# Shifting every right-side SBUF tile of an attention and two-layer kernel by 96 bytes

## The chip, the cores and the metric

The kernel runs on one core of one Trainium2 chip. The metric is the device time of one execution in microseconds (us). Three runs of the kernel before gave 1021.41, 1022.04 and 1022.06 us; the median is 1022.04 us. The profile is of one further execution.

## The reference

The inputs are q, k, v of 4 batches, 8 heads, 576 positions and 64 channels, a vector s per head and position, and two pairs of weights of 512 x 2048 and 2048 x 512. The weights are float64, all else float32, the output too.

```python
cum  = cumsum(max(s, 0))
bias = min(-(cum[:, None] - cum[None, :]), 0)
attn = softmax(where(causal, -1e9, q @ k.T / 8 + bias))
x = (attn @ v) as [2304, 512]
h = x @ w1_in;  x = max(0.01*h, h) @ w1_out            # first layer
h = x @ w2_in;  out = (max(h,0) + log1p(exp(-|h|))) @ w2_out   # second layer
```

## The kernel before

**Attention.** `attention` goes through 16 pairs of heads. TensorE makes scores (L252, L262), VectorE masks them and takes maxima (L281), ScalarE exponentiates (L295), GpSimd divides by the sums (L306), TensorE transposes (L318, L323) and multiplies with V (L354). The result stands in SBUF as `xh` and `xl`: a value rounded to the type that TensorE reads in one pass (float32r), and what the rounding left over. Beside it `Fill` already does part of the first layer for batches whose attention is done, with 288 tokens a chunk (L143 through `h_mm`, L539).

**The two layers.** The main loop at the end takes `steps`: the layer, a group of four blocks of 128 hidden units, a chunk of tokens (512, 512, 256, 512, 512; in the very first group twice 288), and one block `f`. Each step has two parts on TensorE:

- `h_mm` (L143) makes 128 hidden units for the chunk: four slices of the model width, three products each (`hi` with `xh`, `hi` with `xl`, `lo` with `xh`). These 12 matmuls add up in one bank of PSUM. The stationary operand is a weight tile (`wih`, `wil`), the moving one `xh` or `xl`.
- `out_mm` (L651) of three steps earlier multiplies the activations `gh` and `gl` with `woh` and `wol` into four banks of PSUM. In layer 0 the weights are stationary and `gh`, `gl` move (`ops = outs[i][:, :N], ((wh[:, sl], gh), ...`); in layer 1 it is the other way round: a slice of 128 columns of `gh` or `gl` is stationary and the 512 columns of `woh` or `wol` move. A step of 512 tokens has 12 such matmuls, in layer 1 a step of 256 tokens has 6. The first product of two halves goes first, then, with `low`, the four with `gl`.

Between the two ScalarE, VectorE and GpSimd make `gf`, `gh` and `gl` of the hidden units (L605, L610 to L624, L149, L150). They also split the next weights into `hi` and `lo` (`split_w`, L105 to L130). Program order on each engine is the order in which the Python code issues. `later` and `tick` put a piece off by so many half steps.

**Where tiles lie.** A tile pool is a piece of every SBUF partition. Pools without a side are laid upwards from the first free byte, 16,512, which is 129 x 128; pools with `side="right"` are laid downwards from the last one, 229,344, which is 1791 x 128 + 96. All pools here are multiples of 128 bytes long (but for the small `st` tiles on the left), so every left tile of the table starts at a multiple of 128 and every right one at 96 past one.

| tile | side | starts at (bytes) | past a multiple of 512 |
|---|---|---|---|
| `xh`, `xl` | left | 16,512 and 53,376 | 128 |
| `wih`, `wil`, `woh`, `wol` | left | 90,240 to 137,344 | 128 |
| `wm`, `wt` of the weight split | left | 139,392 to 145,536 | 128 |
| `acc` (sum of the layer) | left | 155,776 | 128 |
| `gf`, `t`, `e`, `l` (two layers) | right | 196,576 to 210,912 | 480 |
| `gh`, `gl` (two layers), 4 each | right | 212,960 to 227,296 | 480 |
| `gf`, `o`, `gh`, `gl` of `Fill`, 288 columns | right | 209,120 to 224,096 | 96, 224, 352 or 480 |
| `rawi`, `rawo` during attention; `c0`, `c1`, `bb` at the start | right | 217,056 to 225,248 | 480 or 224 |

A chunk of `xh` starts at a multiple of 1024 bytes within its slice in all steps of 512 or 256 tokens; in the chunks of 288 tokens it starts at multiples of 1152. A slice of 128 columns is 512 bytes.

Of the kernel before, what the change touches and what calls it, by code (L numbers as in the profile page):

```python
# [9 lines left out]
F32 = mybir.dt.float32  # L10
# [7 lines left out]
P = 128  # L18
# [12 lines left out]
def attn_moe_moe(ctx, tc, q, k, v, s, w1i, w1o, w2i, w2o, out):  # L31
# [18 lines left out]
    def pool(name, bufs=1, **kw):  # L50
        return tc.tile_pool(name=name, bufs=bufs, **kw)

    dram = ctx.enter_context(pool("dram", space=bass.MemoryType.DRAM))
    keep = ctx.enter_context(pool("keep"))


    xh = keep.tile([P, KD, NT], F32R, tag="xh", name="xh")
    xl = keep.tile([P, KD, NT], F32R, tag="xl", name="xl")
# [688 lines left out]
```

## Time and profile before

| what | value |
|---|---|
| median of three runs | 1022.04 us |
| span of the profiled execution, first to last instruction | 1020.2 us |
| outside the span (median less span) | 1.8 us |
| TensorE busy (matmuls) | 992.0 us, 97% |
| GpSimd, ScalarE, VectorE busy | 559.2, 536.8, 506.3 us |
| main loop of the two layers | from 276 us on; layer 1's output matmuls from 614 us on |

The span is what the profiler recorded between the first and the last instruction. The time of a run also holds what lies around it. Matmuls overlap in TensorE: one begins before the one ahead of it has ended. So the mean duration of a group is longer than its pace; the pace is read from the starts of matmuls that follow each other in the timeline.

### The profile page before, as it was taken

What the parts mean: (1) busy time and instruction counts of PE and PEld (TensorE: products, weight loads), DVE (VectorE), ACT (ScalarE), POOL (GpSimd) and SP (SyncE); (2) the same over time, 40 slices, a digit from 0 to 9 for tenths busy, and PEclk for the clock granted to TensorE, in tenths of its full rate; (3) what the DMA queues carried; (4) which work ended last, traced back from release to release, by engine and by line L of the source; (5) the groups of instructions that cost most, each with busy time, mean ns of one, the idle gap of its engine ahead of it and who ended that gap; (6) DMA issues with size and microseconds to landing.
All of it is one profiled execution on the core that took longest, in us unless ns stands there. A gap on an engine that the chain in (4) does not pass through costs nothing.

```text
span 1020.2 us, 15105 instructions
## 1 busy us (share of the span) xinstructions
PE 992.0 (97%) x5498; PEld 812.4 (80%) x5498; DVE 506.3 (50%) x1133; ACT 536.8 (53%) x1152; POOL 559.2 (55%) x565
## 2 busy tenths in 40 slices
PE   7889999999999999999999998999999999999998
PEld 4667788888998888888888887888778877888886
DVE  6886665554021312321244158547575767576443
ACT  4877676656355333432444365666645554565452
POOL 6757455434156335533553356667766676667453
PEclk9999999999999999999999999999999999999999
DMA  5422333210252002100220021101210121010202
GB/s 172 135 97 67 113 106 101 93 59 25 73 205 76 22 1 83 63 21 1 83 62 22 16 68 41 42 2 45 80 42 1 42 82 42 1 42 21 83 22 83
DMA packets 38518, 62.04 MB, mean 61 GB/s; under 512 B 2932, under 2 KB 25972, under 8 KB 38444
## 3 DMA queue, kind: packets, MB, share of 16 engines
q1 hardware_dynamic: 38204, 60.74, 18.2%
q8 instruction: 44, 0.72, 0.3%
q10 hardware_dynamic: 240, 0.33, 0.1%
q14 instruction: 30, 0.25, 0.1%
HBM read 52.65 MB, written 8.40 MB: 60 GB/s over the span
## 4 chain that ended last, share of the span: by engine, by line
PE 73%; POOL 10%; DVE 8%; issue 6%; ACT 3%; DMA 0%; DVEq 0%; POOLq 0%; ACTq 0%
PE ps_h L143 30%; PE ps_out L651 27%; PE pt_v L354 4%; PE ps_o L539 4%; PE pt_s L262 4%; POOL t L619 3%; PE pt_t L323 3%; POOL gl L150 2%; POOL wm L120 2%; DVE wm L114 2%; PE pt_s L252 2%; ACT sc L295 1%; DVE wm L111 1%; DVE wm L117 1%; POOL wil L130 1%
## 5 line engine op out<-in xcount | busy, mean ns | idle before, releaser
L150 POOL TENSOR_TENSOR gl<-gf,gh 128x512 fp32r<-128x512 f32 (+2 forms) x148 | 178.3, 1206 | 258.9 <-ACT gh L149 243.4
L143 PE MATMUL ps_h<-xh,wih 128*128 128x512 f32 (+2 forms) x688 | 246.5, 358 | 1.1 <-ACT o L543 0.6
L143 PE MATMUL ps_h<-xl,wih 128*128 128x512 f32 (+2 forms) x688 | 244.7, 356 | 0.0
L143 PE MATMUL ps_h<-xh,wil 128*128 128x512 f32 (+2 forms) x688 | 243.9, 354 | 0.0
L143 PEld LDWEIGHTS ps_h<-xh,wih 128*128 128x128 f32 x688 | 129.4, 188 | 21.5 <-ACT o L543 0.8
L306 POOL TENSOR_SCALAR sc<-sc,st 128x512 f32<-128x512 f32 (+4 forms) x160 | 88.1, 562 | 103.8 <-DVE st L302 61.3
L143 PEld LDWEIGHTS ps_h<-xl,wih 128*128 128x128 f32 x688 | 129.4, 188 | 19.0
L143 PEld LDWEIGHTS ps_h<-xh,wil 128*128 128x128 f32 x688 | 129.4, 188 | 18.5
L662 DVE TENSOR_TENSOR acc<-ps_out,acc 128x512 f32<-128x512 f32 (+1 forms) x114 | 67.7, 655 | 129.1 <-PE ps_out L651 129.1
L149 ACT ACTIVATE gh<-gf 128x512 fp32r<-128x512 f32 (+2 forms) x148 | 85.3, 576 | 82.7 <-DVE gf L624 81.8
L605 ACT ACTIVATE gf<-ps_h 128x512 f32<-128x512 f32 (+2 forms) x68 | 36.7, 539 | 172.1 <-PE ps_h L143 168.2
L651 PE MATMUL ps_out<-woh,gh 128*128 128x512 f32 x288 | 116.2, 403 | 5.8 <-ACT gh L149 3.2
L624 DVE TENSOR_TENSOR gf<-gf,t 128x512 f32<-128x512 f32 (+1 forms) x80 | 56.0, 700 | 127.0 <-POOL t L619 127.0
L111 DVE TENSOR_SCALAR wm<-wm 128x512 f32<-128x512 f32 x64 | 42.1, 658 | 147.3 <-ACT wm L105 140.3
L651 PE MATMUL ps_out<-wol,gh 128*128 128x512 f32 x288 | 115.0, 399 | 0.0
L295 ACT ACTIVATE sc<-sc,st 128x512 f32<-128x512 f32 (+2 forms) x144 | 83.3, 581 | 42.9 <-DVE st L286 22.0
L120 POOL TENSOR_TENSOR wm<-wm,wt 128x512 int32<-128x512 int32 x64 | 88.1, 1377 | 28.0 <-DVE wm L117 28.0
L619 POOL TENSOR_TENSOR t<-e,t 128x512 f32<-128x512 f32 (+1 forms) x80 | 98.3, 1228 | 0.0
L651 PE MATMUL ps_out<-gh,woh 128*128 128x512 f32 (+2 forms) x272 | 97.1, 365 | 0.0
L651 PE MATMUL ps_out<-gh,wol 128*128 128x512 f32 (+2 forms) x272 | 96.6, 364 | 0.0
L281 DVE CUSTOM_DVE_ANT_0 sc<-pt_s,mask 128x512 f32<-128x512 f32 (+2 forms) x144 | 66.7, 480 | 57.2 <-PE pt_t L323 46.1
L651 PE MATMUL ps_out<-woh,gl 128*128 128x512 f32 x288 | 80.6, 397 | 1.2 <-POOL gl L150 1.1
(93 smaller groups left out, 1729.2 us busy)
## 6 DMA issues: line engine op xcount, KB each, us to landing
rawi<-in_moe_w_in SPq DMA_DIRECT2D x32, 512.0 KB
rawo<-in_moe_w_out SPq DMA_DIRECT2D x32, 512.0 KB
V<-in_v SPq DMA_DIRECT2D x16, 320.0 KB
Q<-in_q SPq DMA_DIRECT2D x15, 320.0 KB
K<-in_k SPq DMA_DIRECT2D x16, 288.0 KB
out<-acc SPq DMA_DIRECT2D x18, 256.0 KB
part<-o SPq DMA_DIRECT2D x24, 144.0 KB
acc<-part SPq DMA_DIRECT2D x6, 576.0 KB
```

The source lines that it names most:

```text
L111: nc.vector.tensor_scalar(mf, mf, D_MIN, D_MAX, op0=ALU.max, op1=ALU.min)
L120: nc.gpsimd.tensor_tensor(m, m, t, op=ALU.add)
L143: nc.tensor.matmul(ps, a, b, start=n == 0, stop=n == 3 * KD - 1)
L149: nc.scalar.activation(gh, gf, AF.Copy)
L150: nc.gpsimd.tensor_tensor(gl, gf, gh.bitcast(F32), op=ALU.subtract)
L281: nc.vector.tensor_tensor_reduce(out=self.sc[:, j, c], in0=self.ps[j][:, c], in1=m, scale=-scale, scalar=3.0e38, op0=ALU.add, op1=ALU.min, ...
L295: nc.scalar.activation(x, x, AF.Exp, scale=-1.0, bias=self.stat(0, e), accum_out=self.stat(1, e))
L306: nc.gpsimd.tensor_scalar(x, x, self.stat(2, e), 1.0, op0=ALU.mult, op1=ALU.mult)
L619: nc.gpsimd.tensor_tensor(t, e, t, op=ALU.subtract)
L624: nc.vector.tensor_tensor(gf, gf, t, op=ALU.add)
L651: nc.tensor.matmul(ps, a, b, start=f == 0 and m == 0, stop=f == G - 1 and m == 2)
L662: nc.vector.tensor_tensor(d, o, d, op=ALU.add)
```

## The change

A pool named `edge` is opened on the right side ahead of all others there, and one tile of 128 partitions x 24 float32 (96 bytes) is taken from it. Nothing reads or writes this tile. All later right-side tiles start 96 bytes lower: at multiples of 128. `gh` and `gl` of the two layers start at 384 past a multiple of 512 instead of 480; those of `Fill` at 0, 128, 256 or 384. Left-side tiles stay where they are. Every engine has the same instructions in the same order, with the same waits.

```diff
     dram = ctx.enter_context(pool("dram", space=bass.MemoryType.DRAM))
     keep = ctx.enter_context(pool("keep"))
-
+    edge = ctx.enter_context(pool("edge", side="right"))
+    edge.tile([P, 24], F32, tag="edge", name="edge")
 
     xh = keep.tile([P, KD, NT], F32R, tag="xh", name="xh")
```

## Rows read from the trace of the kernel before

**Rows 1.** The page: span, busy time by engine, the granted TensorE clock.
```profile
span 1020.2 us, 15105 instructions
PE 992.0 (97%) x5498; PEld 812.4 (80%) x5498; DVE 506.3 (50%) x1133; ACT 536.8 (53%) x1152; POOL 559.2 (55%) x565
PEclk9999999999999999999999999999999999999999
```

**Rows 2.** The page: the chain of waits, shares by engine.
```profile
PE 73%; POOL 10%; DVE 8%; issue 6%; ACT 3%; DMA 0%; DVEq 0%; POOLq 0%; ACTq 0%
```

**Rows 3.** Groups by line and shape, TensorE: count, busy us, mean ns, idle before.
```profile
L143 PE MATMUL ps_h<-xl,wih 128*128 128x512 f32 x448 | 175.4, 392 | 0.0
...
L651 PE MATMUL ps_out<-woh,gh 128*128 128x512 f32 x288 | 116.2, 403 | 5.8 <-ACT gh L149 3.2 <-DVE acc L662 2.1 <-ACT acc L660 0.5
L651 PE MATMUL ps_out<-wol,gh 128*128 128x512 f32 x288 | 115.0, 399 | 0.0
...
L651 PE MATMUL ps_out<-gh,woh 128*128 128x512 f32 x192 | 76.3, 398 | 0.0
...
L143 PE MATMUL ps_h<-xl,wih 128*128 128x256 f32 x112 | 31.6, 282 | 0.0
...
L651 PE MATMUL ps_out<-gh,wol 128*128 128x256 f32 x48 | 12.1, 283 | 0.0
```

**Rows 4.** Timeline of TensorE, a step of layer 0: start us, duration us.
```profile
522.00 0.40 PE L143 MATMUL ps_h<-xh,wih 128*128 128x512 f32 x1
...
524.07 0.39 PE L143 MATMUL ps_h<-xh,wih 128*128 128x512 f32 x1
...
524.75 0.40 PE L651 MATMUL ps_out<-gh,woh 128*128 128x512 f32 x1
...
527.57 0.40 PE L143 MATMUL ps_h<-xh,wih 128*128 128x512 f32 x1
```

**Rows 5.** Timeline of TensorE, a step of layer 1.
```profile
803.07 0.40 PE L143 MATMUL ps_h<-xh,wih 128*128 128x512 f32 x1
...
803.76 0.39 PE L143 MATMUL ps_h<-xh,wih 128*128 128x512 f32 x1
...
805.80 0.39 PE L651 MATMUL ps_out<-woh,gh 128*128 128x512 f32 x1
...
808.61 0.40 PE L143 MATMUL ps_h<-xh,wih 128*128 128x512 f32 x1
```

**Rows 6.** Timeline of TensorE, matmuls of 288 columns in `Fill` and just after.
```profile
263.10 0.29 PE L143 MATMUL ps_h<-xh,wih 128*128 128x288 f32 x1
...
267.90 0.30 PE L539 MATMUL ps_o<-gh,woh 128*128 128x288 f32 x1
...
270.40 0.29 PE L539 MATMUL ps_o<-gh,woh 128*128 128x288 f32 x1
...
272.00 0.30 PE L539 MATMUL ps_o<-gh,woh 128*128 128x288 f32 x1
...
277.59 0.29 PE L143 MATMUL ps_h<-xh,wih 128*128 128x288 f32 x1
...
282.33 0.29 PE L651 MATMUL ps_out<-gh,woh 128*128 128x288 f32 x1
...
283.91 0.29 PE L143 MATMUL ps_h<-xh,wih 128*128 128x288 f32 x1
```

**Rows 7.** Groups by line and shape, ScalarE and GpSimd.
```profile
L149 ACT ACTIVATE gh<-gf 128x512 fp32r<-128x512 f32 x112 | 70.3, 628 | 73.4 <-DVE gf L624 72.8
...
L124 ACT ACTIVATE woh<-wm 128x512 fp32r<-128x512 f32 x32 | 20.2, 630 | 49.1 <-POOL wm L120 49.1
...
L150 POOL TENSOR_TENSOR gl<-gf,gh 128x512 fp32r<-128x512 f32 x112 | 150.5, 1345 | 193.4 <-ACT gh L149 190.5 <-PE ps_out L651 3.0
...
L130 POOL TENSOR_TENSOR wil<-wm,wih 128x512 fp32r<-128x512 f32 x32 | 43.7, 1366 | 25.9 <-ACT wih L124 24.4 <-PE ps_h L143 1.5
```

## The prediction

> **What bounds the kernel now.** I read the page's busy times first. TensorE is busy for 992.0 of 1020.2 us and runs at the full granted clock throughout [rows 1]; the other compute engines are busy a little over half the time. The chain of waits says the same: 73% of it is TensorE, and no other engine has more than 10% [rows 2]. The groups by line then show that TensorE hardly waits in the two layers: the largest idle time before a group of output matmuls is 5.8 us, over 288 of them [rows 3]. So a change to the pace of the matmuls themselves reaches the end nearly in full, and what happens on the other engines does not, unless it grows a lot.
>
> The same group table shows what the change may touch. Matmuls of 512 columns have three mean durations, though they have the same shape and count of passes: 392 ns for `h_mm`, 398 ns for `out_mm` in layer 0 and 403 and 399 ns for it in layer 1 [rows 3]. The operands of `h_mm` all lie at multiples of 128 bytes. Those of `out_mm` do not: in layer 0 the moving operand `gh` starts 96 bytes past one, in layer 1 the stationary one does. Since matmuls overlap, I take the pace from starts in the timeline.
>
> - Layer 0: `h_mm` runs from 522.00 to 524.75, `out_mm` from there to 527.57 [rows 4]: 2.75 and 2.82 us for 12 matmuls each, so 229 and 235 ns a matmul. Within `h_mm` the first nine gaps take 2.07 us (230 ns each), the last three 0.68 us (227 ns).
> - Layer 1: `h_mm` 803.07 to 805.80, `out_mm` to 808.61 [rows 5]: 2.73 and 2.81 us, so 228 and 234 ns. The last nine gaps of `h_mm` take 2.04 us, 226.7 ns each.
>
> So there is one even pace, 226.7 ns, into which `h_mm` falls after a while, and a slower one, 234 to 235 ns, in which `out_mm` stays. `out_mm` differs from `h_mm` in two ways only: its operand's place in SBUF, and the four PSUM banks it goes round.
>
> **Which of the two it is.** For the place: layers 0 and 1 use the same order of banks, and `h_mm` after them is the same work. Yet after layer 0, where `gh` moves, `h_mm` takes nine gaps at 230 ns before it is even, while after layer 1, where `gh` is stationary, the disturbance is three gaps, 0.69 us from 803.07 to 803.76, 230 ns each [rows 4, 5]. What was read, not where it was written, decides. Further, matmuls of 288 columns show that a moving operand's address alone changes the pace. Three `h_mm` runs in a row with `xh` at a multiple of 256 bytes take 4.80 us for 36 gaps, 133.3 ns, and three with `xh` 128 past one take 4.74 us, 131.7 ns; all else is alike [rows 6]. After the change, `gh` and `gl` of the layers are 128 past a multiple of 256 bytes, the same class as `xh` and the weights in every 512-column step.
>
> Against the place: at 288 columns the displaced `gh` costs nothing that can be seen. The last output matmuls of `Fill` take 1.60 us for 12 gaps (133.3 ns) in one bank, and the first `out_mm` 1.58 us (131.7 ns) in four banks [rows 6]. At 256 columns the means are 282 and 283 ns [rows 3]. So the cost is one of full 512-column matmuls, and I have no rule that says why.
>
> The Trainium skill speaks against the change here: "SBUF — State Buffer", section "Door 1: The DMA port swizzle", has lines of 16 bytes, with a penalty for each crossing to a new one. As 96 is six such lines, the old places would be as good as the new by it, and the time would stay at 1022.0 us. No row shows lines of 16 bytes; the two classes at 288 columns are 128 bytes apart, a multiple of 16 too, and differ.
>
> **The change part by part.** The tile itself has no instruction, no wait and no transfer: 0. No instruction moves on any queue. What is left is the new address.
>
> *Matmuls of `out_mm`, 512 columns.* Layer 0 has 3 x 192 = 576, that is 48 blocks of 12; layer 1 has 3 x 288 = 864, that is 72 blocks (counts in [rows 3], one of the three products shown for layer 0, two for layer 1). At the even pace a block takes 12 x 226.7 ns = 2.72 us. Layer 0: 48 x (2.82 - 2.72) = 4.8 us saved. Layer 1: 72 x (2.81 - 2.72) = 6.5 us.
>
> *Matmuls of `h_mm`, 512 columns.* If nothing disturbs them before, they run even from the start. There are 448 x 3 / 12 = 112 blocks [rows 3], 48 in layer 0 and 64 in layer 1: 48 x (2.75 - 2.72) + 64 x (2.73 - 2.72) = 1.4 + 0.6 = 2.0 us.
>
> Together 13.3 us. From below I allow that each of these 232 blocks keeps a short disturbance at the change of bank and operand, of the size that `h_mm` has in layer 1, 0.01 us: 232 x 0.01 = 2.3 us, which leaves 11.0. The middle is 12.1; I take 12. What bounds the term on the other side is 0 (no dependence on the place).
>
> *Matmuls of 288 and 256 columns.* In `Fill`, `gh` alternates between the two classes of [rows 6] afterwards: (133.3 + 131.7) / 2 = 132.5 ns against 133.3 now, times 288 matmuls is 0.2 us at most. The others are even already: 0.
>
> *ScalarE, VectorE, GpSimd.* Their tiles move too. A ScalarE copy of 512 columns between two displaced tiles takes 628 ns, between two aligned ones 630; GpSimd's subtraction 1345 against 1366 [rows 7]. So nothing is to be had, and it would be hidden behind TensorE anyway: per step of layer 1 GpSimd has two such passes, 2.7 us, in 5.5 us of TensorE. If TensorE gets 2% faster, its waits for ScalarE and VectorE in layer 1 (5.8 us of idle in [rows 3]) could grow by some tenths: up to 0.5 us, kept for the range.
>
> *Transfers.* `rawi` and `rawo` of the attention stage land 96 bytes lower, well ahead of their use; DMA has 0% of the chain [rows 2]: 0.
>
> Sum: the profiled span of 1020.2 us becomes 1008.2. The median lies 1.8 us over the span, which the change doesn't touch: 1010.0 us.
>
> **Rivals.**
>
> 1. *Nothing happens.* The slower pace of `out_mm` comes from its four banks at 512 columns. For it: 288 and 256 columns show no cost of the place. Against it: the two classes at 288 columns and the different after-effects of the two layers. Time: 1022.0 us.
> 2. *Only one side counts*, the moving or the stationary operand. Layer 0 alone gives 4.8 + 1.4 = 6.2 us, so 1015.8; layer 1 alone 6.5 + 0.6 = 7.1 us, so 1014.9. For it: TensorE reads the two in different ways, and the disturbances after them differ. Against it: the loss per matmul is nearly the same, 8 and 7 ns.
> 3. *Slower.* The new class is worse for `gh`: both streams that TensorE reads, moving and stationary, now start at the same place of a 256-byte block and are read at the same time, and get in each other's way in each of the 1440 output matmuls. At 288 columns the worse class costs 1.6 ns in 132. In proportion that is 2.8 ns of 235 at 512 columns: 1440 x 2.8 = 4.0 us, 1026.0 us. It decides from 1.4 ns a matmul on (2 us in all). Against it: `h_mm` has both operands in that class and is the fastest there is.
>
> **How the numbers follow.** The full effect has a chance of 0.50 (its own range 1008.2, with 13.3 us and a little more, to 1012), one side alone 0.14, nothing 0.27, slower 0.09. The predicted time is 1010. For 8 in 10 the range reaches from 1007.5 to 1022.6: it takes in the full effect, the half and no change, and leaves out the slower case and little more at the lower end. A difference below 0.2% (2.0 us) can't be told from no change in a measurement of this kernel; faster than that 0.64, same 0.27, slower 0.09.
>
> **What would show it.** Right: in the timeline of a step of layer 0 and of layer 1, `out_mm` takes 2.72 to 2.74 us for 12 gaps and `h_mm` after it is even from its first gaps; the mean durations of the 512-column groups of `out_mm` fall from 398 and 403 towards 390; steps of 256 columns, ScalarE and GpSimd stay as they are. If only the layer 0 step is shorter, the moving operand is what counts, if only layer 1's, the stationary one. The prediction is wrong if the 512-column pace of `out_mm` stays at 234 ns, or if the pace improves and the idle time before the output matmuls grows by as much.

## The result and the profile after

The changed kernel takes 1013.45 us (median of five; four of them 1012.21 to 1013.70) against 1022.04 us (1021.19 to 1022.52): a ratio of 0.9914 for these four, 95% interval 0.9901 to 0.9927. That is 8.6 us faster by the medians, where 12 had been forecast. A second measurement of the same kernel, `e1_after` below, gave 1013.23 us and 0.9912 (0.9898 to 0.9925).

The other execution took 4651.93 us, with matmuls about 1300 ns apart for a reason that no row shows (without it the median is 1013.0 us), and since it is the profiled one, the profile of `e1_after` is read here as the profile after.

The page of `e1_after`, as [rows 1]:

```profile
span 1011.7 us, 15105 instructions
PE 981.0 (97%) x5498; PEld 811.8 (80%) x5498; DVE 511.8 (51%) x1133; ACT 535.6 (53%) x1152; POOL 558.0 (55%) x565
PEclk9999999999999999999999999999999999999999
```

The span fell by 8.5 us (1020.2 to 1011.7), TensorE's busy time by 11.0. So TensorE does the same work faster and waits 2.5 us more. VectorE is busy for 5.5 us more than before (506.3 to 511.8); the prediction had no change there. Next the groups of TensorE by line and shape (count, busy us, mean ns, idle before), as [rows 3]; every line number is one higher than before:

```profile
L144 PE MATMUL ps_h<-xl,wih 128*128 128x512 f32 x448 | 174.5, 389 | 0.0
...
L652 PE MATMUL ps_out<-woh,gh 128*128 128x512 f32 x288 | 114.7, 398 | 7.9 <-ACT gh L150 4.1 <-DVE acc L663 2.5 <-ACT acc L661 1.4
L652 PE MATMUL ps_out<-wol,gh 128*128 128x512 f32 x288 | 113.1, 393 | 0.0
...
L652 PE MATMUL ps_out<-gh,woh 128*128 128x512 f32 x192 | 74.8, 390 | 0.0
```

`out_mm` fell from 398 to 390 ns in layer 0 and from 403 and 399 to 398 and 393 in layer 1. The 398 holds the longer matmuls just after waits: in `e8` below, where this group hardly waits, it is 391. The idle time before it grew from 5.8 to 7.9 us. The timeline of a step of layer 0, as [rows 4], and of layer 1, as [rows 5] (start us, duration us), shows the pace:

```profile
518.38 0.39 PE L144 MATMUL ps_h<-xh,wih 128*128 128x512 f32 x1
...
520.42 0.39 PE L144 MATMUL ps_h<-xh,wih 128*128 128x512 f32 x1
...
521.10 0.39 PE L652 MATMUL ps_out<-gh,woh 128*128 128x512 f32 x1
...
523.82 0.39 PE L144 MATMUL ps_h<-xh,wih 128*128 128x512 f32 x1
...
791.16 0.39 PE L144 MATMUL ps_h<-xh,wih 128*128 128x512 f32 x1
...
793.88 0.39 PE L652 MATMUL ps_out<-woh,gh 128*128 128x512 f32 x1
...
796.60 0.39 PE L144 MATMUL ps_h<-xh,wih 128*128 128x512 f32 x1
```

Every block of 12 takes 2.72 us, that is 226.7 ns a matmul: `h_mm` 518.38 to 521.10 and 791.16 to 793.88, `out_mm` 521.10 to 523.82 and 793.88 to 796.60. Within `h_mm` of layer 0 the first nine gaps take 2.04 us, even from the start, where they took 2.07.

To see the whole span, I added up the distances between consecutive starts on TensorE, by kind of matmul. What a distance has beyond the even pace of its shape and 30 ns is put into a row of its own, "waits" (the slower matmuls just after a wait are in it too); the first 30 ns of each such distance stay with its kind. Kinds that the table leaves out changed by 0.1 us at most.

| us in the span | before | `e1_after` | difference |
|---|---|---|---|
| from the first matmul to the first `out_mm` | 277.6 | 278.0 | +0.4 |
| layer 0, `out_mm`, 512 columns (576) | 134.9 | 130.8 | -4.1 |
| layer 0, `h_mm`, 512 columns | 143.4 | 142.0 | -1.4 |
| layer 1, `out_mm` (863) | 202.6 | 197.3 | -5.3 |
| layer 1, `h_mm`, 512 columns | 163.9 | 163.3 | -0.6 |
| layer 1, waits | 11.1 | 13.7 | +2.5 |
| layer 0, waits | 0.0 | 0.0 | 0.0 |

So the pace gave 11.4 us, the waits of layer 1 took 2.5 back. (The first row says nothing of the change: it is 276.9 to 278.0 us in the profiles of the runs below.) Both of this has to be explained: what in the place sets the pace, and where the 2.5 us come from.

### The profile page after: what moved, and what is told of

It reads as the page before. It is cut to its first block, busy times and chain, and to the rows that moved or that the text cites. A ratio compares the mean times of both kernels' runs of the same rounds, so it can differ in the third digit from the quotient of the medians.

```text
span 4649.9 us, 15105 instructions
## 1 busy us (share of the span) xinstructions
PE 4640.8 (100%) x5498; PEld 3112.6 (67%) x5498; DVE 483.7 (10%) x1133; ACT 544.4 (12%) x1152; POOL 547.4 (12%) x565
## 4 chain that ended last, share of the span: by engine, by line
PE 100%; DMA 0%; DVE 0%; ACT 0%; SPq 0%; issue 0%; ACTq 0%
PE ps_h L144 40%; PE ps_out L652 35%; PE pt_s L263 6%; PE pt_v L355 6%; PE pt_t L324 5%; PE ps_o L540 5%; PE pt_s L253 3%; PE pt_t L319 1%; PE pt_t L315 0%; DMA K<-in_k 0%; DVE acc L663 0%; ACT o L544 0%; SPq L162 0%; ACTq L544 0%
## 5 line engine op out<-in xcount | busy, mean ns | idle before, releaser
L144 PE MATMUL ps_h<-xh,wih 128*128 128x512 f32 (+2 forms) x688 | 850.5, 1236 | 0.5 <-ACT o L544 0.5
L144 PE MATMUL ps_h<-xl,wih 128*128 128x512 f32 (+2 forms) x688 | 841.7, 1223 | 0.0
L144 PE MATMUL ps_h<-xh,wil 128*128 128x512 f32 (+2 forms) x688 | 838.9, 1219 | 0.0
L144 PEld LDWEIGHTS ps_h<-xh,wih 128*128 128x128 f32 x688 | 478.5, 695 | 189.6 <-issue 186.9
L144 PEld LDWEIGHTS ps_h<-xl,wih 128*128 128x128 f32 x688 | 482.9, 702 | 181.9 <-issue 181.9
L144 PEld LDWEIGHTS ps_h<-xh,wil 128*128 128x128 f32 x688 | 476.3, 692 | 177.6 <-issue 177.2
L652 PE MATMUL ps_out<-gh,woh 128*128 128x512 f32 (+2 forms) x272 | 402.9, 1481 | 0.0
L652 PE MATMUL ps_out<-gh,wol 128*128 128x512 f32 (+2 forms) x272 | 400.2, 1471 | 0.0
L652 PE MATMUL ps_out<-gl,woh 128*128 128x512 f32 (+2 forms) x272 | 326.4, 1478 | 0.0
L263 PE MATMUL pt_s<-K,Q 64*128 64x512 f32 (+3 forms) x256 | 242.3, 2082 | 4.8 <-DMA K<-in_k 4.8
```

Source lines behind the costliest of these rows:

```text
L144: nc.tensor.matmul(ps, a, b, start=n == 0, stop=n == 3 * KD - 1)
L263: nc.tensor.matmul(self.ps[j][:, c], x[r, t * P:(t + 1) * P], y[r, :(t + 1) * P], start=x is Q[i], stop=x is bq,)
L652: nc.tensor.matmul(ps, a, b, start=f == 0 and m == 0, stop=f == G - 1 and m == 2)
```

## The experiments

Ratios are to the kernel before, run on the same chip beside each kernel (medians 1022.0 to 1022.4 us), with their 95% intervals. "Distance" below is how far `gh` and `gl` of the two layers start from the operand that meets them (`woh`, `wol`, at 128), both taken modulo 256 bytes: 224 - 128 = 96 before, 128 - 128 = 0 after.

**The changed kernel again (`e1_after`).** No edit.

> The changed kernel once more, for a trace at the usual clock (in the first profile of it TensorE ran at about a quarter of its pace throughout). If the place of the operands is what counted, out_mm of 512 columns takes 2.72 to 2.74 us for 12 gaps in both layers, the time is about 1013 us, and the rest of the 12 us that were forecast is to be found in idle time or in a pace between 227 and 234 ns. If only one operand counts, the block of one layer is still at 2.81 to 2.82 us.

1013.23 us, 0.9912 (0.9898 to 0.9925), its profile as read above.

**Layer 0 alone back at its old place (`e2_layer0_off`).** `gh` and `gl` of layer 0 start 96 bytes further, at 224 modulo 256; those of layer 1 stay aligned.

```diff
-    def g_parts(gp, gf, N, width):
-        gh = gp.tile([P, width], F32R, tag="gh", name="gh")[:, :N]
+    def g_parts(gp, gf, N, width, o):
+        gh = gp.tile([P, width + 64], F32R, tag="gh", name="gh")[:, o:o + N]
...
-        gs[n] = g_parts(gpool, gf, N, 512)
+        layer = steps[n][0]
+        gs[n] = g_parts(gpool, gf, N, 512, 24 if layer == 0 else 0)
```

> All right-side tiles at multiples of 128 bytes, but gh and gl of layer 0 (there the moving operand) are put 96 bytes further inside wider tiles, so that they are 224 past a multiple of 256 as in the kernel before. If the moving operand's place counts: layer 0 out_mm back at 2.82 us a block, layer 1 as in the changed kernel, and the time 4 to 6 us over the changed kernel's. If only the stationary one counts: as the changed kernel, within 1 us. If neither (the gain came from tiles of the other engines): as the changed kernel too, and the next run as well.

1019.16 us, 0.9968 (0.9956 to 0.9981), 5.9 us over the changed kernel. Timeline: a block of `out_mm` and the `h_mm` after it, first layer 0, then layer 1:

```profile
519.48 0.40 PE L653 MATMUL ps_out<-gh,woh 128*128 128x512 f32 x1
...
522.30 0.40 PE L144 MATMUL ps_h<-xh,wih 128*128 128x512 f32 x1
...
793.93 0.39 PE L653 MATMUL ps_out<-woh,gh 128*128 128x512 f32 x1
...
796.65 0.39 PE L144 MATMUL ps_h<-xh,wih 128*128 128x512 f32 x1
```

2.82 us in layer 0, as before; 2.72 in layer 1, as after. Added up, layer 0 is back to the hundredth (134.91 and 143.38 us), layer 1's `out_mm` keeps its 5.3 us and `h_mm` its 0.6, and the waits in layer 1 are 13.5 us. So those waits grow with layer 1's own pace, whether layer 0 is fast or not.

**Layer 1 alone back at its old place (`e3_layer1_off`).** The same edit with `layer == 1`.

> The same for layer 1, where gh and gl are the stationary operand: only they are 96 bytes further. If the stationary operand's place counts: layer 1 out_mm back at 2.81 us a block, time 4 to 7 us over the changed kernel's. If only the moving one counts: as the changed kernel, within 1 us.

1015.87 us, 0.9937 (0.9924 to 0.9951). The same two blocks:

```profile
520.02 0.39 PE L653 MATMUL ps_out<-gh,woh 128*128 128x512 f32 x1
...
522.74 0.39 PE L144 MATMUL ps_h<-xh,wih 128*128 128x512 f32 x1
...
793.94 0.39 PE L653 MATMUL ps_out<-woh,gh 128*128 128x512 f32 x1
...
796.74 0.40 PE L144 MATMUL ps_h<-xh,wih 128*128 128x512 f32 x1
```

2.72 us in layer 0, 2.80 in layer 1. This is 2.6 us over the changed kernel where 4 to 7 were expected: the waits in layer 1 are back at 11.3 us, near the 11.1 before, and give 2.4 us back. Against the kernel before, the two halves gain 0.0063 and 0.0032, together 0.0095, where the whole gains 0.0088: they add up within the intervals. The moving side (layer 0) and the stationary side (layer 1) both count, and layer 0 keeps all it gains, since it has no waits that could grow.

**All right-side tiles at multiples of 128, but 128 from their partners (`e4_edge224`).** With a tile of 224 bytes `gh` and `gl` start at 0 modulo 256, the weights still at 128.

```diff
-    edge.tile([P, 24], F32, tag="edge", name="edge")
+    edge.tile([P, 56], F32, tag="edge", name="edge")
```

> The edge tile is 224 bytes instead of 96: right-side tiles of the two layers start at multiples of 256 (256 past one of 512) instead of 128 past one. If 128 bytes is all that counts: as the changed kernel, 1013 us. If the class within 256 bytes counts as it does at 288 columns (1.6 ns in 132 for the class at 0): out_mm blocks 1% longer than in the changed kernel, time 2 to 4 us over it. If a read of 512 columns from a multiple of 256 touches fewer pieces and that counts: faster than the changed kernel, up to 5 us.

1020.78 us, 0.9984 (0.9975 to 0.9993): 7.5 us over the changed kernel, more than any of the three readings had.

```profile
523.72 0.40 PE L652 MATMUL ps_out<-gh,woh 128*128 128x512 f32 x1
...
526.51 0.39 PE L144 MATMUL ps_h<-xh,wih 128*128 128x512 f32 x1
...
798.91 0.40 PE L652 MATMUL ps_out<-woh,gh 128*128 128x512 f32 x1
...
801.70 0.40 PE L144 MATMUL ps_h<-xh,wih 128*128 128x512 f32 x1
```

2.79 us in both layers. That all tiles begin at multiples of 128 bytes is as true here as in the changed kernel, and nearly nothing is gained: it is not that by itself which helps.

**Both sides at multiples of 256 (`e5_both256`).** The same 224 bytes on the right, and 128 bytes on the left, so that `gh`, `gl`, the weights and `xh` all start at 0 modulo 256.

```diff
+    keep.tile([P, 32], F32, tag="left", name="left")
...
-    edge.tile([P, 24], F32, tag="edge", name="edge")
+    edge.tile([P, 56], F32, tag="edge", name="edge")
```

> The right side as in the run with 224 bytes (gh, gl at multiples of 256), and the left side moved up by 128 bytes, so that xh, xl and all weights are at multiples of 256 too. If it counts that the moving and the stationary operand start alike within 256 bytes: 226.7 ns a matmul of 512 columns everywhere, blocks of 2.72 us, time 1012 to 1014 us as the changed kernel's. If 128 past a multiple of 256 is good by itself and 0 is bad: h_mm gets slow as well, blocks of 2.75 to 2.80 us throughout, time 1024 to 1032 us.

1013.26 us, 0.9912 (0.9899 to 0.9926), the changed kernel's time.

```profile
515.49 0.39 PE L653 MATMUL ps_out<-gh,woh 128*128 128x512 f32 x1
...
518.21 0.39 PE L145 MATMUL ps_h<-xh,wih 128*128 128x512 f32 x1
...
788.41 0.39 PE L653 MATMUL ps_out<-woh,gh 128*128 128x512 f32 x1
...
791.13 0.39 PE L145 MATMUL ps_h<-xh,wih 128*128 128x512 f32 x1
```

2.72 us in both. `e4` and `e5` have the same place of `gh`; only the partner moved. What counts in these runs is that the two operands start alike modulo 256 bytes, not where either of them lies. They need not be alike modulo 512: in the changed kernel `gh` is at 384 and `woh` at 128. One thing these runs can't tell apart: all of `gh` and `gl` share one place and all weights another, so it may be a matmul's own two operands that must be alike, or the moving one and the weights that are loaded for the next matmul meanwhile (weight loads, PEld, are busy for 80% of the span beside the 97% of the matmuls).

**Distances of 64 and 32 bytes (`e6_edge32`, `e7_edge64`).** `gh` and `gl` start at 192 and at 160 modulo 256.

```diff
-    edge.tile([P, 24], F32, tag="edge", name="edge")
+    edge.tile([P, 8], F32, tag="edge", name="edge")
```

(In `e7` it is `[P, 16]`.)

> The edge tile is 32 bytes: gh and gl are 192 past a multiple of 256, which is a multiple of 64, against 128 for their partners. If alike within 64 bytes is enough: 2.72 us a block, time about 1013 us. If alike within 256 is needed: blocks of 2.78 to 2.82 us, time 1019 to 1023 us.

> The edge tile is 64 bytes: gh and gl are 160 past a multiple of 256, a multiple of 32 and 32 bytes from their partners. If alike within 32 bytes is enough: 2.72 us a block, about 1013 us. If alike within 256 is needed: 2.78 to 2.82 us, 1019 to 1023 us. If only the distance from the partner counts and a short one costs little: between the two.

1019.99 us, 0.9979 (0.9970 to 0.9988), and 1020.77 us, 0.9987 (0.9978 to 0.9996). First `e6`, then `e7`:

```profile
523.00 0.40 PE L652 MATMUL ps_out<-gh,woh 128*128 128x512 f32 x1
...
525.76 0.40 PE L144 MATMUL ps_h<-xh,wih 128*128 128x512 f32 x1
...
798.01 0.40 PE L652 MATMUL ps_out<-woh,gh 128*128 128x512 f32 x1
...
800.81 0.39 PE L144 MATMUL ps_h<-xh,wih 128*128 128x512 f32 x1
```

```profile
523.43 0.40 PE L652 MATMUL ps_out<-gh,woh 128*128 128x512 f32 x1
...
526.23 0.40 PE L144 MATMUL ps_h<-xh,wih 128*128 128x512 f32 x1
...
798.52 0.39 PE L652 MATMUL ps_out<-woh,gh 128*128 128x512 f32 x1
...
801.32 0.39 PE L144 MATMUL ps_h<-xh,wih 128*128 128x512 f32 x1
```

2.76 and 2.80 us, 2.80 and 2.80 us. All four other distances that were tried lose most of the gain:

| distance, bytes | kernel | block of 12 in layer 0, us | in layer 1, us | ratio |
|---|---|---|---|---|
| 0 | `e1`, `e5` | 2.72 | 2.72 | 0.9912 |
| 32 | `e7` | 2.80 | 2.80 | 0.9987 |
| 64 | `e6` | 2.76 | 2.80 | 0.9979 |
| 96 | before | 2.82 | 2.81 | 1 |
| 128 | `e4` | 2.79 | 2.79 | 0.9984 |

It is not a ramp: 32 bytes cost about as much as 128. Why 64 is a little better in layer 0 stays open.

**The waits: another bank for the output (`e8_banks_2_6`).** On the changed kernel, one PSUM bank is moved from `h_mm` to `out_mm`, so that an output bank has one more step to be emptied in.

```diff
-    ps_h = ctx.enter_context(pool("ps_h", bufs=3, space=PSUM))
-    ps_o = ctx.enter_context(pool("ps_o", bufs=5, space=PSUM))
+    ps_h = ctx.enter_context(pool("ps_h", bufs=2, space=PSUM))
+    ps_o = ctx.enter_context(pool("ps_o", bufs=6, space=PSUM))
```

> The changed kernel with two PSUM banks for h_mm instead of three, and six for out_mm instead of five. If the idle time that grew in layer 1 is waits of out_mm for banks that VectorE or ScalarE have yet to empty (1.4 us at each of two places): the wait moves from the third to the fifth matmul of a block and 0.4 us each are saved at some four places, time 1 to 2 us under the changed kernel's. If the waits are for gh and gl alone, nothing changes; if two banks are too few for h_mm, it gets 1 to 5 us slower, in steps of 256 columns first.

1019.14 us, 0.9972 (0.9963 to 0.9981): 5.9 us slower than the changed kernel, a little more than the worst case that was expected. Groups of TensorE:

```profile
L144 PE MATMUL ps_h<-xh,wih 128*128 128x512 f32 x448 | 176.5, 394 | 11.7 <-DVE gf L621 11.7
...
L652 PE MATMUL ps_out<-woh,gh 128*128 128x512 f32 x288 | 112.7, 391 | 0.7 <-ACT acc L661 0.4 <-ACT gh L150 0.3
```

The waits before this group of `out_mm` go from 7.9 to 0.7 us, as meant, and come back as 11.7 us before `h_mm`, whose bank VectorE has not read yet (L621). Waits in layer 1 are 19.8 us in all. The pace of `out_mm` stays even with six banks as with five.

**The waits: the layer change (`e9_spread`).** At the change of layer VectorE makes four slices of `xl` (L594) in one piece ahead of the `gf` that the next `out_mm` needs. Timeline of VectorE in `e1_after`, and the matmul that waits for it:

```profile
613.22 0.42 DVE L112 TENSOR_SCALAR wm<-wm 128x512 f32<-128x512 f32 x1
...
615.11 0.69 DVE L118 SCALAR_TENSOR_TENSOR wm<-rawi,wm 128x512 int32<-128x512 int32 x1
615.71 5.75 DVE L594 TENSOR_TENSOR xl<-acc,xh 128x512 fp32r<-128x512 f32 x4
621.39 0.68 DVE L625 TENSOR_TENSOR gf<-gf,t 128x512 f32<-128x512 f32 x1
...
622.78 0.80 PE L652 MATMUL ps_out<-woh,gh 128*128 128x512 f32 x1 [2.82 <-ACT gh L150]
```

In `e9` each slice is a piece of its own, one per step, and the first comes a step later.

```diff
-            later(1, split_x, slice(c0, c0 + N))
+            for kk in range(KD):
+                later(2 + kk, split_x, slice(c0, c0 + N), kk)
```

> The changed kernel, with the split of layer 0's result into xh and xl put off by a step and spread over four steps, one slice in each, instead of four slices at once. In the changed kernel TensorE stands still for 3.0 us at the change of layers and then runs nine matmuls at half pace (4.6 us in all), while VectorE does four such slices in 5.75 us ahead of what the next output matmuls need. If this idle time is a chain on VectorE that no pace of TensorE shortens: it goes, and the time is 3 to 5 us under the changed kernel's. If it is the longer chain of layer 1 itself, the first step of which has no cover: it stays, within 1 us.

1015.93 us, 0.9943 (0.9930 to 0.9957): 2.7 us slower than the changed kernel, which neither reading had. Timelines of VectorE and then TensorE:

```profile
619.21 1.79 DVE L593 TENSOR_TENSOR xl<-acc,xh 128x512 fp32r<-128x512 f32 x1 [2.65 <-ACT xh L592]
620.92 0.68 DVE L624 TENSOR_TENSOR gf<-gf,t 128x512 f32<-128x512 f32 x1
...
622.32 0.50 PE L651 MATMUL ps_out<-woh,gh 128*128 128x512 f32 x1 [3.57 <-ACT gh L150]
```

The slice at the head of VectorE's queue now waits 2.65 us for ScalarE's half of the same slice (`xh`, L592), and the `gf` behind it waits along: 3.6 us on TensorE where it was 2.8. Cut apart and put off, the slices make this wait longer; since the run changed both, it doesn't show which of the two does.

**The waits: when the weights are split (`e10_plan`, `e11_plan_spread`, `e12_plan2`).** `when` lists the steps at which the pieces of the next group's weights are split on VectorE, ScalarE and GpSimd (L106 to L131); `a` is the group's first step. `e10` and `e12` move the first four by one to four steps; `e11` is `e10` with the edit of `e9`.

```diff
-        when = [a + 2, a + 5, a + 8, a + 11, z - 3, z, z - 1, z + 2]
+        when = [a + 1, a + 3, a + 12, a + 14, z - 3, z, z - 1, z + 2]
```

(In `e12` the first four are `a + 4, a + 6, a + 12, a + 15`.)

> The changed kernel, with the four early splits of the next group's weights at steps 1, 3, 12 and 14 of a group instead of 2, 5, 8 and 11, so that VectorE doesn't have them just ahead of the additions that empty the PSUM banks, nor in the short steps of 256 tokens. If the idle time that grew in layer 1's groups is output matmuls waiting behind such work on VectorE, ScalarE and GpSimd: 3 to 7 of the 9 us of these waits go. If the waits only move to the new places: the same time as the changed kernel's, within 2 us.

> Both together. If the two kinds of idle time are separate, the gains add up: 1001 to 1007 us, under the kernel before by 1.5 to 2%. If they share a cause, it is no better than the better one of the two.

> The changed kernel, with the four early splits at steps 4, 6, 12 and 15 of a group. In the run with 1, 3, 12 and 14 the idle time at the second and third chunk of a group was gone, but new and longer idle time stood at its first chunk, where the last splits of the group before are still under way (their steps 0 and 2 of the new group). If it is the neighbourhood of those splits that made it worse: the old idle time is gone and no new one comes, 4 to 6 us under the changed kernel's, 1007 to 1009 us. If each step with a split costs idle time wherever it stands: 1013 us or more.

`e10`: 1018.02 us, 0.9963 (0.9950 to 0.9975). `e11`: 1024.55 us, 1.0027 (1.0017 to 1.0036), slower than the kernel before. `e12`: 1011.06 us (1010.65 to 1011.42), 0.9891 (0.9874 to 0.9907), the fastest of all here. Waits in layer 1, added up as above: 18.0, 24.2 and 11.3 us, against 13.7 in the changed kernel. The expectations were missed: `e10` is 4.8 us slower than the changed kernel where 3 to 7 us of gain or no change were expected, `e11` is worse than either of its parts, and `e12` gains 2.2 us, between its two readings. The intervals of the ratios of `e12` and `e1` overlap; the single times do not (1010.65 to 1011.42 and 1012.42 to 1013.70). The largest wait of `e10`, and below it VectorE and TensorE of `e12` at the layer change and its largest wait elsewhere:

```profile
819.62 0.80 PE L652 MATMUL ps_out<-woh,gh 128*128 128x512 f32 x1 [3.76 <-DVE acc L663]
```

```profile
612.56 4.67 DVE L594 TENSOR_TENSOR xl<-acc,xh 128x512 fp32r<-128x512 f32 x4
617.15 0.68 DVE L625 TENSOR_TENSOR gf<-gf,t 128x512 f32<-128x512 f32 x1
...
619.14 0.39 PE L652 MATMUL ps_out<-woh,gh 128*128 128x512 f32 x1
...
845.23 0.50 PE L652 MATMUL ps_out<-woh,gh 128*128 128x512 f32 x1 [2.23 <-ACT gh L150]
```

In `e12` VectorE begins `xl` 3.2 us earlier (612.56 for 615.71), of which 2.5 are the weight piece (`rawi`, 613.22 to 615.71 in `e1_after`) that no longer stands ahead of it, and the `out_mm` of 619.14 has nothing to wait for. Other waits appear (2.2 us at 845.23). So the order of the other engines' work sets these waits: from 24.2 to 11.3 us with the same pace of matmuls. What stands ahead at each place was looked at only at the layer change.

## Why the prediction held, and what it mis-sized

**The mechanism held.** TensorE bounds the kernel, and the place of the operands in SBUF set the pace of the 512-column `out_mm`. The even pace of 226.7 ns, taken from the last gaps of `h_mm` before [rows 4, 5], is what the blocks of `out_mm` shown above have after. The rest of `h_mm` became even too: 1.4 us in layer 0 and 0.6 in layer 1, as forecast.

**The pace term was 0.6 us too large.** 11.4 us came, where the blocks had added up to 13.3 and 12 was taken. Layer 0's `out_mm` gave 4.1 us, not 4.8, and layer 1's 5.3, not 6.5. The step read one block of each layer to 0.01 us, 2.82 and 2.81, where the mean over all matmuls was 134.9 / 576 = 234.2 ns, that is 2.81 a block, in layer 0, and the mean after is 227.1 ns, not 226.7. In layer 1 it went from 234.7 to 228.6 ns, in which the first 30 ns of each wait are counted (31 waits before, 35 after); the matmuls without a wait went from 234.0 to 227.5 ns. The 0.2 us allowed for `Fill` did not show.

**The waits were the larger error.** The prediction saw 5.8 us of waits, before one group, where layer 1 had 11.1 in all. It kept up to 0.5 us for their growth, in the range only; it was 2.5. Here the argument from shares failed: the other engines were half idle, but between two points at which `out_mm` waits for them the time is theirs. What TensorE gains there it waits at the next such point. The runs show that link: with layer 1 fast the waits are 13.5 to 13.8 us (`e1`, `e2`, `e5`), with layer 1 slow 11.1 to 11.6 (before, `e3`, `e4`, `e6`, `e7`), wherever the tiles of the other engines lie. From 700 us on, past the layer change, they are 8.5 to 8.7 and 6.5 to 6.9 us. VectorE's longer busy time is not the cause: in `e2` and `e5` it is 507.6 and 508.7 us, with the same waits. Of the 5.9 us that layer 1's matmuls gained, 2.5 went back into waits (0.1 to 0.5 us at each of nine places). Layer 0 has no such waits and kept its 5.5 us. A term of 2.5 us in place of none, and 11.4 in place of 12, makes 8.9; less the 0.4 us up to the first `out_mm` that is the 8.5 of the span.

**The rivals.** *Nothing happens, the four banks are at fault*: refuted, `out_mm` is even in four banks with five or six buffers. *Only one side counts*: refuted by `e2` and `e3`, each of which keeps the part of the layer that is left aligned. *Slower, since both operands at the same place of a 256-byte block get in each other's way*: refuted, and the opposite is so. Of the five distances tried, 0 is the only one with an even pace (`e1`, `e5`), and the others cost 1.5 to 3.7% a block (2.76 to 2.82 us for 2.72).

**What the prediction had right for a wrong reason.** It spoke of `gh` joining "the same class" as the weights, and read the classes as places of one operand. `e4` shows that a class of its own is worth nothing: at multiples of 256 bytes, beside weights at 128 past one, `gh` is nearly as slow as before. The 288-column rows fit this as well: the weights lie at 128 past a multiple of 256, and the faster `xh` (131.7 ns against 133.3) is the one that also lies there [rows 6]. In `e5` the weights lie at 0 and the two places of `xh` have changed sides, yet the same stretches take 4.80 us (263.29 to 268.09) and 4.74 us (277.81 to 282.55), as before: the class of `xh` alone does not set them. But the two stretches also differ in the PSUM banks they write, so all else was not alike, and no run changed the distance there alone.

**The rule that spoke against.** The Trainium skill, "SBUF — State Buffer", section "Door 1: The DMA port swizzle", has lines of 16 bytes. By it the places tried here, all multiples of 32 bytes, should have been alike. The trace disagrees: blocks of 2.72 us at distance 0 and of 2.76 to 2.82 at 32, 64, 96 and 128 bytes.

What stays open is why TensorE is faster with the two alike: no run looked at it from inside.

## What to carry to other kernels

Where TensorE bounds a kernel and its float32r matmuls of 512 columns have different paces for the same shape, compare the start addresses of the moving and the stationary operand modulo 256 bytes, and shift one pool until they are alike; here that gave 0.9% for one tile of 96 bytes. Multiples of 128 on one side alone are worth little. Before adding up such a gain, look for the places where the bounding engine already waits: what is gained between two of them may be waited away, and the order of the other engines' work is then worth a look (here 2.2 us more, from 1013.23 to 1011.06).

## What the runs showed beside this

**The clock after the wait at the layer change.** In `e1_after` the matmuls that follow this wait (622.78, above) are slower, and the granted clock of that stretch is lower. Second, the stretch in `e1_after`, the kernel before and `e3` (stretch, its length, busy times by engine, granted clock, DMA share, GB/s); third, the wait in `e3`:

```profile
623.38 0.63 PE L652 MATMUL ps_out<-wol,gh 128*128 128x512 f32 x1
...
625.94 0.46 PE L652 MATMUL ps_out<-wol,gh 128*128 128x512 f32 x1
```

```profile
621.00:627.00 6.00, 4.22 (x12) 3.37 (x13) 3.63 (x7) 3.29 (x6) 2.72 (x3) 0.72 0.00 0
...
627.00:633.00 6.00, 4.99 (x15) 3.98 (x16) 2.86 (x6) 4.03 (x7) 3.50 (x3) 0.72 0.00 0
...
621.00:627.00 6.00, 5.30 (x23) 4.33 (x24) 2.55 (x5) 4.29 (x8) 3.81 (x4) 1.00 0.00 0
```

```profile
621.70 0.50 PE L653 MATMUL ps_out<-woh,gh 128*128 128x512 f32 x1 [2.62 <-ACT gh L150]
```

From 623.38 to 625.94 six matmuls take 2.56 us, 427 ns each where the even pace is 227; the clock of the stretch has a mean of 0.72, so part of it was at the lower level of 1.2 GHz. The kernel before has the same (0.72), so this is not part of the gain, and the full clock throughout that the prediction read from the tenths of the page [rows 1] was not quite so.

The wait does not always bring it: `e3` waits 2.6 us at the same place, and its clock stays at 1.00, as it does in `e4` and `e6`. Nor does the slow stretch come on top of the rest. Among the runs with a slow layer 1, those with the low clock here (before, `e7`) lose 1.4 to 1.5 us to the slower matmuls and 0.4 to 0.5 at the next waits, some 30 us later; those without (`e3`, `e4`, `e6`) lose 0.1 and then 1.9 to 2.0. The sum is 1.9 to 2.0 us in all five: what TensorE gains by the clock, too, it waits away at the next waits.

**Narrow matmuls behave otherwise.** At 256 columns the output blocks of layer 0 take 1.44 us (mean, from starts) at distance 96, 1.43 at 0 and 128, and 1.41 and 1.42 at 32 and 64, so being alike is not the best there.
